# An inverse transform's first half runs ahead of the fourth block of the next forward transform

## The chip, the cores and the metric

The kernel runs on one core of one Trainium2 chip. The metric is the device time of one execution in microseconds; of several runs the median is given. Engines are named as in the profile: PE is TensorE (PEld its weight loads), DVE is VectorE, ACT is ScalarE, POOL is GpSimd, and SP is SyncE, which here only issues DMAs. TensorE's granted clock is full throughout the stretches that matter here.

## The reference, cut to what matters

There are 8 sequences of 3072 positions with 256 channels. Each goes through a circular convolution by way of the frequency domain, and the result, taken as 24,576 tokens, goes through a top-1 mixture of 8 experts, each with a capacity of 768 tokens; tokens beyond it give zero rows.

```
X = np.fft.rfft(x, axis=1);  Y = X * (filt_r + 1j * filt_i)
y = np.fft.irfft(Y, n=3072, axis=1)
tok = y.reshape(24576, 256);  logits = tok @ w_gate;  e = argmax(logits)
# the first 768 tokens of each expert are kept, in order of position
h = maximum(kept[e] @ w1[e], 0);  out[token] = softmax(logits)[e] * (h @ w2[e])
```

All data is float32.

## The kernel before, in words

**Stages.** The tokens that fill all experts come from the first three batches, so the kernel convolves three batches and then runs the experts, with a branch behind it for data where that doesn't do. The convolution of a batch has four parts. The *forward transform* (`a_rows` for the second and third batch) multiplies the input by a constant matrix A; the *middle* (`Conv.middle`) forms products with a second constant matrix out of Q (`bm`), multiplies them by the filter on VectorE and GpSimd (`b`), turns them back and adds the gate's columns on TensorE (`g`), and applies a third matrix (`bi`) into the tile V; VectorE then transposes V in four quarters (`ti`); and the *inverse* (`ai`) multiplies V by AI, evicts each result on ScalarE into a tile rt, copies the 8 gate columns into L on GpSimd, and stores the tile to ybuf in HBM by SyncE.

**The hand-over** between two batches, which happens twice, is the stretch that the change touches. In it the program issues, in this order on each engine: the forward transform of the next batch for the group of 64 frequencies (`rows_in(0)`, four blocks, called R64 in the diff), the inverse's first half (`halves[0]`, nine steps of up to three tiles of 136 columns), the forward transform for the 32 other frequencies (`rows_in(1)`, two blocks), and the inverse's second half (`halves[1]`, six steps S[0] to S[5]). Each block of `a_rows` is 64 matmul records, evicted by ScalarE in two parts into four columns of Q, from where DMAs store it to `zturn` in HBM: two of 256 KB per block by GpSimd for the 64, four of 128 KB per block by SyncE for the 32. The four blocks use columns 8 to 23 of Q, the two blocks columns 16 to 23 again. `load_Q` then brings zturn back into Q in another layout, four columns a load, six loads by SyncE; the loads 0 to 3 need all stores of the 64, the loads 4 and 5 those of the 32.

**The routing** of a batch (`route`) needs L complete: `counts` (f0 to f5, VectorE), `sums` (f6, a few small matmuls on TensorE), `slots` (f6b to f12, VectorE), then three masks (`onehot`, VectorE) and three tables (`table`, TensorE, each needs its mask and adds into one bank). It is woven by hand between the inverse's second half and the next batch's middle. The lists `fill` and `ahead` are what the next `middle` runs between its own steps: `ahead` gives one item after each `b` but the first, `fill` one list at a time.

**What sets the order.** The schedule is manual: each engine and each DMA queue does its work in the order of the program, and waits only on data and buffers. The tile rt has seven buffers, the PSUM banks for results are seven in rotation, and the masks have two buffers. A write into columns of Q waits until DMAs that read them have landed. In the second hand-over, the weights of the first expert begin to load as well (`load_a`, behind S[3] in SyncE's queue), through the tile raw and ScalarE.

Of the kernel before, what the change touches and what calls it, by code (L numbers as in the profile page):

```python
# [9 lines left out]
F32 = mybir.dt.float32  # L10
# [21 lines left out]
def dft_constants():  # L32
# [18 lines left out]
    th = tp * ((n2[:, None] * k2[None, :]) % 32) / 32  # L51
    C, S = np.cos(th), np.sin(th)
    std = np.zeros((2, 32, 2, 32))
    std[0, :, 0], std[1, :, 0], std[0, :, 1], std[1, :, 1] = C, S, -S * cj, C * cj
    inv = np.zeros((2, 32, 2, 32))
    inv[0, :, 0], inv[1, :, 0], inv[0, :, 1], inv[1, :, 1] = C.T, (-S * cj).T, S.T, (C * cj).T
    sp, isp = np.zeros((2, 32, 2, 32)), np.zeros((2, 32, 2, 32))
# [36 lines left out]
def fftconv_moe_kernel(ctx, tc, x, x0, fr, fi, fny, wg, w1, w2, ca, cai, cb, co, out, cap):  # L94
    nc = tc.nc
# [21 lines left out]
    ybuf = dram.tile([NB0, NTS, 128, CH], F32, name="ybuf")  # L117
    yall = dram.tile([NB, NTS, 128, CH], F32, name="yall")
    zturn = dram.tile([4 * NP, N2, D], F32, name="zturn")
# [3 lines left out]
    def bank():  # L123
        return psum.tile([128, 512], F32, name="ps", tag="ps")
# [45 lines left out]
    def run(fs):  # L170
        for f in fs:
            f()

    class Conv:
# [108 lines left out]
        def a_rows(self, part, t0):  # L283

            rows, r0 = PARTS[part]
            o = (8, 16)[part] + t0
            k, z = 128 // rows, self.Q[:, o:o + 4, :]
            for h in range(2):
                ps = bank()
                for i in range(2):  # L290
                    for j in range(k):
                        c, t = divmod(j * NT1[part] + t0 + 2 * h + i, 4)
                        nc.tensor.matmul(ps[j * rows:(j + 1) * rows, i * D:(i + 1) * D], self.Ac[c][:, t * QP + r0:t * QP + r0 + rows],  # L293
                                         self.xts[c][:, t, :], start=True, stop=True)
                nc.scalar.copy(z[:, 2 * h:2 * h + 2, :].rearrange("p t d -> p (t d)"), ps)
            for j in range(k):
                n2 = j * NT1[part] + t0
                (nc.sync if part else nc.gpsimd).dma_start(out=zturn[r0:r0 + rows, n2:n2 + 4, :], in_=z[j * rows:(j + 1) * rows])

        def load_Q(self, p, n):  # L300

# [124 lines left out]
        v = V[q // parts][:, q % parts * n:(q % parts + 1) * n].rearrange("p a t e -> p a e t")  # L426
        nc.vector.transpose(v, v)

    def ai(V, dst, h, L=None, parts=(1, 0)):

        c0, w = HS[h]
        k = 512 // w

        def step(part, j0, n):
            rows, r0 = PARTS[part]
            ps = bank()
            for i in range(n):
                for s in range(128 // rows):
                    o = s * NT1[part] + j0 + i
                    nc.tensor.matmul(ps[s * rows:(s + 1) * rows, i * w:(i + 1) * w], AI[:, o, r0:r0 + rows], V[h][:, :w // 2, o, :],  # L440
                                     start=True, stop=True)
            rt = p1b.tile([128, 512], F32, name="rt", tag="rt", bufs=7)
            nc.scalar.copy(rt[:, :n * w], ps[:, :n * w])  # L443
            rv = rt[:, :n * w].rearrange("p (t c) -> p t c", c=w)
            if h == 0:
                t0 = part * NT1[0] + j0
                nc.gpsimd.tensor_copy(L[:, t0:t0 + n, :], rv[:, :, 128:136])
            nc.sync.dma_start(out=dst[part * NT1[0] + j0:part * NT1[0] + j0 + n, :, c0:c0 + w].rearrange("t p c -> p t c"), in_=rv)

        return [lambda part=part, j0=j0: step(part, j0, min(k, NT1[part] - j0)) for part in parts for j0 in range(0, NT1[part], k)]  # L450
# [8 lines left out]
    def new_V(pool):  # L459
        return [pool.tile([128, n // 2, N2, 2], F32, name=f"V{c}") for c, n in VS]  # L460
# [385 lines left out]
    p1b = base_ctx.enter_context(tc.tile_pool(name="p1b", bufs=1))  # L846
# [5 lines left out]
    cv = Conv(p1b, top, side, True)  # L852
    route_tiles(p1b)

    with tc.manual_schedule():

        V = new_V(vp)
# [36 lines left out]
        fill, ahead = [[cv.finish_low]], [lambda: (cv.t(3), cv.t(4)), lambda: None, lambda: cv.t(5)]  # L894
        nz = -(-len(zfill) // (NB0 - 1))

        def with_zeros(fill, at):
            fill = [list(f) for f in fill] + [[] for _ in range(10 - len(fill))]
            for i in range(len(at)):
                fill[at[i]].append(lambda: zero_out(1))  # L900
            return fill

        def rows_in(part):
            return [lambda t0=t0: cv.a_rows(part, t0) for t0 in range(0, NT1[part], 4)]

        loads = []
        for b in range(NB0 - 1):
            fill = with_zeros(fill, (5, 6, 8) if b == 0 else (7,))
            order = [[6, 7], [], [0, 4], [1, 5], [2, 3]] if b == 0 else [[], [6, 7], [0, 4], [1, 5], [2, 3]]
            for i, cs in enumerate(order):  # L910
                fill[i] += loads[:1] + [lambda b=b, c=c: cv.load_x(b + 1, c) for c in cs]
                loads = loads[1:]
            cv.middle(V, fill, ahead)
            L = new_L()
            halves = [ai(V, ybuf[b], h, L) for h in range(2)]
            counts, sums, slots, masks, table = route(L, False, (ohp, ohp))
            Q = [lambda p=p: cv.load_Q(p, 4) for p in range(0, NP, 4)]
            for q in range(4):
                ti(V, q)
            run(rows_in(0))  # L920
            S = halves[0]
            run(S[:5] + [Q[0]] + S[5:8] + [Q[1]] + S[8:])
            interleave(rows_in(1), counts)
            S = halves[1]
            S[0]()
            sums()
            if b + 2 == NB0:
                side_ctx.close()
                w0 = run_ctx.enter_context(tc.tile_pool(name="w0", bufs=1, side="right"))
                raw0 = run_ctx.enter_context(tc.tile_pool(name="raw0", bufs=1, side="right"))  # L930
                ep = run_ctx.enter_context(tc.tile_pool(name="ep", bufs=1, side="right"))
                (load_a, cut_a), (load_b, cut_b) = (load_part(0, part, raw0, w0, 4) for part in "ab")
            run(slots)
            run([Q[2], masks[0], S[1], S[2], masks[1], Q[3], S[3], table[0]])
            if b + 2 == NB0:
                load_a()
            ahead = S[4:]
            fill = [[table[1]], [masks[2]], table[2:]]
            loads = Q[4:]


        b = NB0 - 1
# [21 lines left out]
        fill = [f + g for f, g in zip(fill + [[]] * (len(more) - len(fill)), more)]  # L964
# [11 lines left out]
        L = new_L(True)  # L976
        counts, sums, slots, masks, table = route(L, True, (ohp, ohp))
# [85 lines left out]
        with tc.If(least < cap):  # L1063
            with ExitStack() as gp:
                sm["group"] = "again"
                p1b = gp.enter_context(tc.tile_pool(name="gbase", bufs=1))
# [6 lines left out]
                V = new_V(p1b)  # L1073
# [7 lines left out]
                with tc.For_i(0, NB, 1) as b:  # L1081
# [10 lines left out]
                    L = new_L()  # L1092
                    dst = yall[bass.ds(b, 1)].rearrange("o t p c -> (o t) p c")
                    for h in range(2):
                        run(ai(V, dst, h, L))
                    counts, sums, slots, masks, table = route(L, False, (gside, gside))
# [68 lines left out]
```

## Time and profile before

| what | value |
|---|---|
| median of 3 runs | 483.5 us (481.23 to 485.53) |
| the profiled execution's own time | 478.28 us |
| its span, first to last instruction | 476.4 us |
| PE busy | 455.8 us (96%) |
| DVE, ACT, POOL busy | 242.5, 251.5, 206.8 us |
| mean granted clock of TensorE | 0.996 |
| DMA, whole span | 108.30 MB, 227 GB/s |

The busy share says how long an engine had an instruction in flight; where it stood idle, the trace names what it waited for, in brackets behind the instruction that came next. Times in the trace are from the span's start. A DMA's line shows when it was issued; its landing is listed by itself.

### The profile page before, as it was taken

The numbers are of one execution on the slowest core, as the hardware profiler recorded it, in microseconds if no ns is written. First come the engines' busy times: TensorE is split into PE (matmuls) and PEld (weight loads), VectorE is DVE, ScalarE is ACT, GpSimd is POOL, SyncE is SP. The second block draws the span as 40 slices with busy tenths as digits, with TensorE's granted clock in tenths as the row PEclk, the third lists the DMA queues.
The fourth block names the chain that finished last, engine by engine and source line by source line (L and its number), as shares of the span: only waits on it lengthen the run. The fifth ranks groups of instructions, "written<-read, shape, count | busy, mean of one in ns | idle before, by whom it ended". The sixth has DMA issues, their size and how long they took to land.

```text
span 476.4 us, 10559 instructions
## 1 busy us (share of the span) xinstructions
PE 455.8 (96%) x4125; PEld 437.9 (92%) x4125; DVE 242.5 (51%) x562; ACT 251.5 (53%) x586; POOL 206.8 (43%) x259
## 2 busy tenths in 40 slices
PE   8999997899968999998999999999999999999994
PEld 8999876899758899998999999999999999999994
DVE  4587758777578788875432432422422422423500
ACT  3555754357542887654365582582572662773411
POOL 3074240642405675247423743552561561662022
PEclk9999999999999999999999999999999999999998
DMA  8999788994899975838465989989989989993001
GB/s 316 355 296 349 283 251 270 301 250 178 239 272 300 239 164 107 227 90 167 157 156 166 200 227 274 378 190 274 373 200 276 379 201 283 364 168 97 1 25 49
DMA packets 69260, 108.30 MB, mean 227 GB/s; under 512 B 4848, under 2 KB 44496, under 8 KB 69072
## 3 DMA queue, kind: packets, MB, share of 16 engines
q1 hardware_dynamic: 51536, 72.71, 47.4%
q0 software_dynamic: 16352, 32.71, 30.8%
q10 hardware_dynamic: 1312, 2.10, 1.4%
q8 instruction: 35, 0.57, 0.5%
q14 instruction: 25, 0.20, 0.1%
HBM read 61.11 MB, written 46.40 MB: 226 GB/s over the span
## 4 chain that ended last, share of the span: by engine, by line
PE 71%; issue 9%; DMA 7%; DVE 4%; ACT 3%; POOL 3%; SPq 1%; POOLq 0%; ACTq 0%
PE ps L636 23%; PE ps L687 23%; PE ps L368 5%; PE ps L335 5%; PE ps L382 4%; PE ps L293 3%; DMA raw<-w 3%; PE ps L277 3%; PE ps L440 3%; DMA ybuf<-rt 3%; POOL y L693 2%; PE ps L610 1%; DMA V<-x 1%; DMA rows<-ybuf,idxg 1%; PE ps L322 1%
## 5 line engine op out<-in xcount | busy, mean ns | idle before, releaser
L687 PE MATMUL ps<-wbh,h 128*128 128x256 f32 x768 | 139.4, 282 | 0.0
L619 DVE SCALAR_TENSOR_TENSOR h<-ps,h 128x384 fp32r<-128x384 f32 x128 | 66.8, 552 | 106.3 <-ACT h L617 106.1
L687 PEld LDWEIGHTS ps<-wbh,h 128*128 128x128 f32 x768 | 119.1, 189 | 0.8 <-issue 0.4
L687 PE MATMUL ps<-wbl,h 128*128 128x256 f32 x384 | 107.7, 280 | 0.0
L693 POOL DMA_INDIRECT y<-ob,idxs x48 | 48.1, 1002 | 117.9 <-ACT ob L690 99.4
L636 PE MATMUL ps<-xl,wah 128*128 128x384 f32 x256 | 86.2, 337 | 0.3 <-DVE xl L621 0.2
L636 PE MATMUL ps<-xh,wah 128*128 128x384 f32 x256 | 86.3, 337 | 0.0
L636 PE MATMUL ps<-xh,wal 128*128 128x384 f32 x256 | 86.0, 336 | 0.0
L617 ACT ACTIVATE h<-ps 128x384 fp32r<-128x384 f32 x128 | 58.7, 498 | 32.9 <-PE ps L636 32.3
L687 PEld LDWEIGHTS ps<-wbl,h 128*128 128x128 f32 x384 | 72.7, 189 | 0.0
L690 ACT ACTIVATE ob<-ps,gt 128x256 f32<-128x256 f32 x48 | 22.7, 475 | 86.9 <-PE ps L687 47.3
L355 POOL TENSOR_TENSOR t<-t,t 128x256 f32<-128x256 f32 x33 | 25.2, 763 | 56.3 <-DVE t L351 44.9
L636 PEld LDWEIGHTS ps<-xl,wah 128*128 128x128 f32 x256 | 48.1, 188 | 0.9 <-DVE xl L621 0.9
L636 PEld LDWEIGHTS ps<-xh,wah 128*128 128x128 f32 x256 | 48.1, 188 | 0.2
L636 PEld LDWEIGHTS ps<-xh,wal 128*128 128x128 f32 x256 | 48.1, 188 | 0.0
L596 POOL DMA_INDIRECT rows<-ybuf,idxg x42 | 42.4, 1009 | 12.8 <-issue 11.6
L368 PE MATMUL ps<-IG,t 128*128 128x136 f32 x288 | 39.0, 282 | 1.6 <-POOL t L356 0.7
L621 DVE TENSOR_TENSOR xl<-ps,xh 128x384 fp32r<-128x384 f32 x32 | 16.2, 547 | 43.8 <-ACT xh L617 43.8
L371 ACT CAST yh<-ps 128x408 fp32r<-128x408 f32 x48 | 23.8, 504 | 27.4 <-PE ps L368 24.0
L368 PEld LDWEIGHTS ps<-IG,t 128*128 128x128 f32 x288 | 35.5, 190 | 2.9 <-POOL t L356 1.6
L335 PE MATMUL ps<-Bc,Q 128*128 128x128 f32 x288 | 36.5, 278 | 0.0
L443 ACT COPY rt<-ps 128x408 f32<-128x408 f32 (+3 forms) x40 | 20.3, 514 | 27.1 <-PE ps L440 19.7
(141 smaller groups left out, 739.7 us busy)
## 6 DMA issues: line engine op xcount, KB each, us to landing
y<-zt SPq DMA_DIRECT2D x12, 2048.0 KB, 21.7
raw<-w SPq DMA_DIRECT2D x13, 1024.0 KB, 9.7
wbl<-w POOLq DMA_DIRECT2D x16, 512.0 KB, 10.3
wal<-w POOLq DMA_DIRECT2D x14, 512.0 KB, 5.7
Q<-zturn SPq DMA_DIRECT2D x12, 512.0 KB, 6.0
ZA<-x SPq DMA_DIRECT2D x12, 384.0 KB, 12.4
zturn<-Q POOLq DMA_DIRECT2D x16, 256.0 KB, 4.5
ybuf<-rt SPq DMA_DIRECT2D x16, 256.0 KB, 5.4
```

The source lines that it names most:

```text
L335: nc.tensor.matmul(ps[:, i * 128:(i + 1) * 128], self.Q[:, p, h * 128:(h + 1) * 128], self.Bc[:, 1 if p == NP - 1 else 0, :], start=True, ...
L355: eng.tensor_tensor(out=t1[:, :, 0, :], in0=t1[:, :, 0, :], in1=t2[:, :, 1, :], op=ALU.subtract)
L368: nc.tensor.matmul(ps[:, i * 136:(i + 1) * 136], self.ysb[(p // 4, h)][:, (p % 4) * 128:(p % 4 + 1) * 128], self.IG[:, h, :], start=True, ...
L371: nc.scalar.copy(fh[:, o], ps[:, :408])
L443: nc.scalar.copy(rt[:, :n * w], ps[:, :n * w])
L596: nc.gpsimd.indirect_dma_start(out=rows[:, t, :], out_offset=None, in_=yrows[:lim, :], in_offset=bass.IndirectOffsetOnAxis(ap=idx[:, j + t ...
L617: nc.scalar.activation(out=hi, in_=ps, func=AF.Relu if relu else AF.Copy)
L619: nc.vector.scalar_tensor_tensor(out=lo, in0=ps, scalar=0.0, in1=hi.bitcast(F32), op0=ALU.max, op1=ALU.subtract)
L636: nc.tensor.matmul(ps[:, :n * 128], w[:, kk, m * 128:(m + 1) * 128], y[:, kk, o], start=k == 0, stop=k == 5)
L687: nc.tensor.matmul(ps[:, :D], y[:, m, o], w[:, m, :], start=m == 0 and j == 0, stop=m == NF - 1 and j == 2)
L690: nc.scalar.activation(out=ob, in_=ps[:, :D], func=AF.Copy, scale=gt[:, i:i + 1])
L693: ins = nc.gpsimd.indirect_dma_start(out=out, out_offset=bass.IndirectOffsetOnAxis(ap=(idxs if ix is None else ix)[:, j:j + 1], axis=0), i ...
```

## The change

The first half of the inverse is issued after three of the four blocks of 64 instead of after all four. Its first two tiles are evicted into columns 4 to 7 of Q, which the second load of Q fills later, instead of into rt. The stores of the blocks of 32 are issued by GpSimd as well. The first two loads of Q are issued behind the forward transform. The sums come ahead of S[0], S[4] moves ahead of the next middle, and the third mask moves to the place behind the first table.

```
-                (nc.sync if part else nc.gpsimd).dma_start(out=zturn[r0:r0 + rows, n2:n2 + 4, :], in_=z[j * rows:(j + 1) * rows])
+                nc.gpsimd.dma_start(out=zturn[r0:r0 + rows, n2:n2 + 4, :], in_=z[j * rows:(j + 1) * rows])
...
-    def ai(V, dst, h, L=None, parts=(1, 0)):
+    def ai(V, dst, h, L=None, parts=(1, 0), stage=()):
...
+        stage = list(stage)
...
-            rt = p1b.tile([128, 512], F32, name="rt", tag="rt", bufs=7)
+            rt = stage.pop(0) if stage else p1b.tile([128, 512], F32, name="rt", tag="rt", bufs=7)
...
-            halves = [ai(V, ybuf[b], h, L) for h in range(2)]
+            stage = [cv.Q[:, k:k + 2, :].rearrange("p k d -> p (k d)") for k in (4, 6)]
+            halves = [ai(V, ybuf[b], h, L, stage=() if h else stage) for h in range(2)]
...
-            run(rows_in(0))
-            S = halves[0]
-            run(S[:5] + [Q[0]] + S[5:8] + [Q[1]] + S[8:])
+            R64 = rows_in(0)
+            run(R64[:3] + halves[0] + R64[3:])
             interleave(rows_in(1), counts)
             S = halves[1]
-            S[0]()
-            sums()
+            run([Q[0], sums, S[0], Q[1]])
...
             run(slots)
-            run([Q[2], masks[0], S[1], S[2], masks[1], Q[3], S[3], table[0]])
+            run([S[1], masks[0], Q[2], S[2], masks[1], S[3], Q[3], table[0], masks[2], S[4]])
             if b + 2 == NB0:
                 load_a()
-            ahead = S[4:]
-            fill = [[table[1]], [masks[2]], table[2:]]
+            ahead = S[5:]
+            fill = [[table[1]], [], table[2:]]
             loads = Q[4:]
```

## Rows read from the trace of the kernel before

**Rows 1.** Windows: stretch, length, busy us (records) of PE, PEld, DVE, ACT, POOL; clock.
```profile
56.20:92.10 35.90, 31.52 (x477) 25.79 (x476) 26.21 (x50) 15.95 (x33) 12.72 (x27) 1.00 0.86 247
116.10:153.00 36.90, 31.57 (x477) 25.82 (x476) 26.33 (x50) 15.86 (x33) 12.59 (x27) 1.00 0.83 245
...
220.00:424.00 204.00, 204.00 (x1541) 202.68 (x1540) 72.06 (x191) 112.20 (x211) 97.64 (x95) 1.00 0.90 250
```

**Rows 2.** TensorE's waits, whole span: us in total, times, longest.
```profile
PE pr L576 <- DVE ohh L568: 6.7, 4, 1.7
PE pr L515 <- DVE ends L508: 3.0, 2, 2.0
...
PE ps L368 <- DVE yl L372: 0.6, 1, 0.6
```

**Rows 3.** Timeline of TensorE, first hand-over: start, us, what, [idle before, releaser].
```profile
56.29 3.88 PE L293 MATMUL ps<-ZA,A 96*64 96x256 f32 x33
...
63.35 5.97 PE L440 MATMUL ps<-V,AI 128*32 128x136 f32 x128
...
72.72 1.06 PE L440 MATMUL ps<-V,AI 128*32 128x128 f32 x32
74.83 0.17 PE L515 MATMUL pr<-ends,tri 128*128 128x8 f16 x1 [1.04 <-DVE ends L508]
...
75.05 3.00 PE L440 MATMUL ps<-V,AI 128*32 128x128 f32 x64
79.67 0.52 PE L576 MATMUL pr<-ohh,ol 128*128 128x96 f16 x8 [1.62 <-DVE ohh L568]
80.03 2.01 PE L335 MATMUL ps<-Bc,Q 128*128 128x128 f32 x16
...
90.62 0.51 PE L576 MATMUL pr<-ohh,ol 128*128 128x96 f16 x8 [1.72 <-DVE ohh L568]
90.97 1.12 PE L335 MATMUL ps<-Bc,Q 128*128 128x128 f32 x8
```

**Rows 4.** Timeline of VectorE, first hand-over.
```profile
59.08 2.50 DVE L427 STREAM_TRANSPOSE V<-V 128x2176 f32<-128x2176 f32 x1
...
72.06 0.35 DVE L483 TENSOR_REDUCE mx<-L 128x24 f32<-128x192 f32 x1 [6.08 <-POOL L L447]
...
75.16 0.17 DVE L523 COPY bs<-pr 128x16 f32<-128x16 f32 x1 [0.31 <-PE pr L518]
...
78.39 0.36 DVE L566 TENSOR_TENSOR ohh<-ioh,hif 128x384 f16<-128x384 f16 x1
```

**Rows 5.** Timeline of ScalarE, the eighth tile of the half.
```profile
70.74 0.50 ACT L443 COPY rt<-ps 128x408 f32<-128x408 f32 x1 [1.81 <-DMA ybuf<-rt]
```

**Rows 6.** Timeline of GpSimd, first hand-over.
```profile
64.36 1.03 POOL L298 DMA_DIRECT2D zturn<-Q x2 [0.71 <-ACT Q L295]
...
71.84 0.19 POOL L447 COPY L<-rt 128x8 f32<-128x8 f32 x1 [0.34 <-ACT rt L443]
82.65 0.72 POOL L355 TENSOR_TENSOR t<-t,t 128x256 f32<-128x256 f32 x1 [10.62 <-DVE t L351]
```

**Rows 7.** Timeline of SyncE's queue: the first load of Q.
```profile
70.35 1.16 SPq L303 DMA_DIRECT2D Q<-zturn  x1
```

**Rows 8.** Line L298, first hand-over: landing of GpSimd's eight stores of 256 KB.
```profile
DMA to landing us min/median/max: 3.9/4.6/5.0
```

**Rows 9.** Line L303, whole span: landing of the twelve loads of Q, 512 KB.
```profile
DMA to landing us min/median/max: 4.5/6.0/9.3
```

**Rows 10.** DMA issues, second hand-over, 124.7 to 124.9: count, KB, landing.
```profile
zturn<-Q POOLq DMA_DIRECT2D x2, 256.0 KB, 6.0
```

**Rows 11.** Timeline of TensorE, second hand-over.
```profile
135.67 0.17 PE L515 MATMUL pr<-ends,tri 128*128 128x8 f16 x1 [1.97 <-DVE ends L508]
```

**Rows 12.** Timeline of ScalarE, behind the second hand-over.
```profile
154.59 0.62 ACT L756 CAST wah<-raw 128x512 fp32r<-128x512 f32 x1 [5.20 <-DMA raw<-w]
```

**Rows 13.** Line L764, whole span: accumulating DMAs issued by GpSimd, ns min/median/max.
```profile
L764 POOL DMA_DIRECT2D wbl<-w x16: 1273/1299/1975, 171.2 to 423.4; - x16
```

## The prediction

> **What bounds the kernel now.** I read the windows first, then the waits of TensorE, then one hand-over between batches engine by engine. The windows [rows 1] show a kernel in which TensorE does not stop: from 220 to 424 us it is busy 204.00 of 204.00 us, so whatever is won earlier arrives at the end undiminished, and only TensorE's idle time can be won. The two hand-overs are where it idles: 4.4 us in the first stretch and 5.3 us in the second. The waits [rows 2] say for whom: 6.7 us in four waits of the slot table for a mask, and 3.0 us in two waits of the sums for the counts, all on VectorE. That is 9.7 us, 2.0% of the span, and is the ceiling of what this change can give. VectorE is not overloaded there: it stands idle for 6.08 us and starts the counts late, at 72.06, because the last gate column is copied at 71.84 [rows 4, 6]. That copy is late because ScalarE waited 1.81 us at its eighth tile for a store to release a buffer [rows 5].
>
> **The change, part by part, in the first hand-over.**
>
> *The inverse's first half before the fourth block.* TensorE runs the four blocks from 56.29 to 63.35, 1.76 us each [rows 3]. After three it is at 61.6; the half needs the second transpose, which starts at 59.08 and takes 2.50 [rows 4], so it starts at about 61.7. This edit costs 0.1. The half takes 5.9 (5.97 with its last matmul's tail [rows 3]) and ends at 67.6; the fourth block fills 67.6 to 69.4, and the two blocks of 32 frequencies end at 72.8 where they ended at 72.72. No matmul is added.
>
> *The two tiles in the operand.* Nine tiles against seven buffers became a wait; nine against nine leave none. No instruction is added. The last tile leaves ScalarE at about 68.3 and its gate column is copied by 68.6, against 72.03. The counts take 72.06 to 74.83, 2.8 us [rows 3, 4], so they end at 71.4, ahead of TensorE. The sums run at 72.8 without a wait: 1.04 us gone.
>
> *Sums before the half's first step.* The sums take 0.2, the next four steps of the second half 1.06 plus 3.0 (75.05 to 79.67 less the wait of 1.62) [rows 3]. TensorE is through at 77.1. VectorE begins the slots 0.33 after the sums (74.83 to 75.16) and the table follows 4.5 later (75.16 to 79.67) [rows 3, 4]: 77.7. So 0.6 of the 1.62 us remains. What is late next is again the mask.
>
> *The fifth step and the third mask.* The fifth step moves ahead of the next batch's first products; it costs its own 1.05 there and gives it back behind them. The third mask (1.2 us, 78.39 to 79.67 for such a one with its table's start [rows 3, 4]) moves into a stretch where VectorE has no product to form yet, since the first of them come at T, below. The wait of 1.72 before 90.62 [rows 3] goes. TensorE is then ready for the first products at 77.7 + 0.36 + 1.05 = 79.1, with that step done.
>
> *What becomes late: the first load of Q.* It needs the fourth block's stores. GpSimd issued them 2.75 us after the block's start (61.6 to 64.36 [rows 3, 6]); now that is 70.35, the second of the two 0.52 later, at 70.9. Landing took 3.9 to 5.0 in the first hand-over [rows 8] and 6.0 for the last two in the second [rows 10]. I take 4.3, below the median of 4.6, because the half's nine stores were issued from 63 on and are nearly through. SyncE issues the load at about 75.2 where it issued it at 70.35 [rows 7]. Loads of Q land after 4.5 to 9.3, median 6.0 [rows 9]; I take 4.8, nearest the shortest, which also was a first load. So the products start at **T = 80.1** and TensorE idles 1.0 us: the wait taken away comes back here in part.
>
> *The same landing holds ScalarE.* The last block of 32 writes the columns of Q that the fourth block's stores are reading, so its two evictions wait from about 72 to 75.2, with five evictions of the inverse behind them on ScalarE at 0.5 to 0.6 each. TensorE has seven banks and needs the first of the blocked ones only at T, so it doesn't feel this. SyncE does: the store of the first step, in front of the second load, goes out at about 77, the load at 77.5. Landing after 6.0 is 83.5; TensorE wants it at T + 2.0 + 1.05 = 83.1. I charge 0.4.
>
> *All stores by GpSimd.* Eight stores of 128 KB leave SyncE's queue and cost GpSimd 8 x 0.52 = 4.2 us [rows 6]. GpSimd was idle 10.62 us there, until 82.65 [rows 6]. The second four wait for ScalarE, go out from 76.6 to 78.7, and end before its next product at about 82.6. Nothing for that, as long as an issue stays near 0.52. The nearest dear row is an issue with accumulation, up to 1.98 [rows 13]; that is a rival below.
>
> **The sum.** The second table's last product ended at 90.97 + 1.12 = 92.1 [rows 3]. From the first product, at 80.03, that is 12.1 us, less the wait of 1.72 and the step's 1.05: 9.3. Now it ends at T + 9.3 + 0.4 = 89.8: **2.3 us gained**. The second hand-over is the same but waited 1.97 for the sums where the first waited 1.04 [rows 3, 11]: **3.2 us**. There the weights of the first expert are loaded too; ScalarE waited 5.20 us for them [rows 12] and passed 0.6 us on to TensorE [rows 2]. SyncE issues that load earlier when eight stores are gone; I take 0.5 of the 0.6. Total 6.0 of the execution's own 478.28 us (span 476.4 and 1.9 around it), 1.25%. The median of the runs, 483.5, stands 1.1% above that execution; the same share makes **477.4**.
>
> By the Trainium skill ("DMA: Bandwidth & Descriptors", Anatomy of one DMA) a transfer takes some 2 us plus its bytes at 436 GB/s; with that, an estimate, the stores would land at 74.1 and the load at 77.4, before TensorE is ready, and the sum would be that of the case "all in time" below. The landings of 3.9 and more for 256 KB [rows 8] speak against it in this stretch.
>
> **The rivals.**
>
> *All in time (0.13).* Both landings at their shortest: 70.9 + 3.9 + 4.5 = 79.3, next to TensorE's 79.1. The gains are 3.5 and 4.4, with the weights 0.6: 8.5 us, 474.9. For it: the queue is emptier than when those rows were taken. Against: the fourth block's stores share the engines with the tail of the half's.
>
> *The waits only change places (0.22).* The landings of the second hand-over: 70.9 + 6.0 + 6.0 = 82.9 for T. The first hand-over then ends at 92.2 and gains nothing, the second gains 0.8: about 482.7 us. For it: 6.0 is the median of such loads and was seen for those very stores. Against: both are rows of a queue with other stores in front.
>
> *GpSimd's issues drag (0.05).* At 1.98 [rows 13] the eight stores hold GpSimd from 72 to 88, while the next products need four subtractions and additions of 0.72 [rows 6] on it before TensorE's group at T + 5.4 = 85.5. That group then starts at about 90.8, 5.3 late; 2.6 us lost in the first and 1.7 in the second, 487.8. Against: beside the transposes such issues took 0.52 [rows 4, 6]. The Trainium skill has this as a rule ("SBUF — State Buffer", SBUF: two separate sides): while VectorE runs an operation in a two-port mode, GpSimd can't write the descriptors of its DMAs. No row here shows a stretched issue of this kind of store, so its chance is small.
>
> *The load is the bound (0.08), slower.* One mechanism: the first load, queued so late, meets the first step's store, the 32s' stores and the next loads, and lands after the longest 9.3 [rows 9] behind stores at 6.0: T = 86.2. The first hand-over ends at 95.5, 3.4 later, the second 2.5 later: 5.9 us, 489.5. It loses from T = 83.3 on, and by over 1% from 85.7. Against: the loads that took that long were issued together behind other traffic.
>
> That the edit has no effect isn't open: the buffer count decides the wait [rows 5], and the order of issue is the program's.
>
> **The numbers.** The forecast has 0.52. This kernel's measurement tells about 1% (4.8 us) from no change; the forecast's own range, T from 79.4 to 81.2, is 7.4 to 3.8 us of gain, and I count 0.05 of its chance as under 1%. Faster: 0.52 + 0.13 - 0.05 = 0.60; within 1%: 0.05 + 0.22 + 0.05 = 0.32; slower: 0.08. The range goes from all in time, with 1.5 us for the spread of the runs (481.23 to 485.53), to the case of changed places: 473.2 to 483.5.
>
> **What would show it.** In the changed trace the sums should have no wait, ScalarE none for the inverse's buffers, and the table one wait of about 0.6 us and none at the third mask. A new wait of about 1 us should stand before the first products, ended by the load of Q, and one of about 3 us on ScalarE before the last block of 32, ended by a store. The counts should start at 68.6, the first load at about 75.2. If the load is issued after 77 or takes over 6, the gain is gone; if GpSimd's issues of stores exceed 1 us, the third rival holds.

## The result, and the profile after

The changed kernel takes 484.89 us in the median of 20 runs, the kernel before 482.33 in 20 runs on the same chip. The ratio is **1.0051, with a 95% interval of 1.0031 to 1.0071**: half a per cent slower where 1.25% of gain was forecast, and above the range. (Disturbed executions are left out of every ratio here; in e12 that leaves four runs.) The profiled execution took 486.63 us with a span of 484.8, but it can't be set against that of before as a whole: its first hand-over begins at 59.38 where the other's began at 56.29 [rows 3], 3.09 us lost in the start-up, which the change does not touch. So I compare by stage, from the first matmul of a hand-over to the end of the last table's product (the third table, which the prediction's sum calls the second).

The windows of the changed kernel (stretch, length, busy us and records of PE, PEld, DVE, ACT, POOL; clock, DMA share, GB/s) are the first hand-over, a stretch inside it, and the second one:

```profile
59.30:95.80 36.50, 32.70 (x476) 26.56 (x475) 25.47 (x48) 15.75 (x33) 16.53 (x34) 0.95 0.85 235
84.70:89.90 5.20, 4.47 (x32) 3.88 (x33) 2.58 (x4) 0.59 (x1) 2.53 (x4) 0.67 0.99 296
120.00:158.60 38.60, 33.01 (x475) 27.32 (x475) 25.34 (x48) 15.76 (x33) 16.27 (x34) 0.96 0.85 237
```

Against [rows 1] one thing is new: TensorE's granted clock, 1.00 in both hand-overs before, is 0.95 and 0.96, and in the stretch behind the first products 0.67, a mixture of the two levels (from 87.20 to 89.30 it is 0.50 throughout, 1.2 of 2.4 GHz). The DMA engines, which were near full before (0.86, 0.83), are as full now. The rows also say where the time went: in the two hand-overs together TensorE stands idle for 9.4 us (length less busy time) where it stood for 9.7, but it is busy for 65.7 us where it was for 63.1, with the same matmuls.

TensorE's waits, whole span (us in total, times, longest), against [rows 2]:

```profile
PE ps L335 <- DMA Q<-zturn: 6.0, 3, 3.2
...
PE pr L577 <- DVE ohh L569: 1.5, 2, 0.7
PE ps L368 <- DVE yl L372: 1.3, 1, 1.3
PE ps L441 <- issue: 1.1, 1, 1.1
...
PE ps L335 <- ACT rt L444: 0.7, 1, 0.7
```

The 6.7 us of waits for masks have become 1.5, and the 3.0 us for the counts are gone, as forecast. In their place stand 6.0 us for loads of Q, 0.7 for an eviction at the second load, and 1.1 inside the inverse's half of the second hand-over ("issue": the trace shows nothing that TensorE waited for there). So 8.2 us of one kind are taken away and 7.8 of other kinds stand in their place, with a lower clock behind them.

TensorE's timeline in the first hand-over, to be read beside [rows 3]:

```profile
64.83 5.96 PE L441 MATMUL ps<-V,AI 128*32 128x136 f32 x128
...
76.04 0.18 PE L516 MATMUL pr<-ends,tri 128*128 128x8 f16 x1
...
80.89 0.52 PE L577 MATMUL pr<-ohh,ol 128*128 128x96 f16 x8 [0.74 <-DVE ohh L569]
...
84.72 2.57 PE L335 MATMUL ps<-Bc,Q 128*128 128x128 f32 x16 [2.28 <-DMA Q<-zturn]
87.21 1.98 PE L441 MATMUL ps<-V,AI 128*64 128x128 f32 x16
89.91 1.13 PE L335 MATMUL ps<-Bc,Q 128*128 128x128 f32 x8 [0.72 <-ACT rt L444]
...
94.47 0.51 PE L577 MATMUL pr<-ohh,ol 128*128 128x96 f16 x8
94.82 1.12 PE L335 MATMUL ps<-Bc,Q 128*128 128x128 f32 x8
```

The half starts 5.45 us after the hand-over's first matmul, the sums and the last table have no wait, and the first table waits 0.74. Then TensorE stands for 2.28 us, and its next two groups take 2.57 and 1.98 us where the same work took 2.01 and 1.10 before, at the lower clock of the window above.

The other engines at the same place, answering to [rows 4 to 7]: VectorE's counts, ScalarE's last block of 32, GpSimd's stores, SyncE's first two loads.

```profile
71.57 0.35 DVE L484 TENSOR_REDUCE mx<-L 128x24 f32<-128x192 f32 x1 [2.49 <-POOL L L448]
...
79.33 1.07 ACT L295 COPY Q<-ps 128x512 f32<-128x512 f32 x2 [4.24 <-PE ps L441]
...
73.45 1.07 POOL L298 DMA_DIRECT2D zturn<-Q  x2 [1.92 <-ACT Q L295]
...
80.70 1.93 POOL L298 DMA_DIRECT2D zturn<-Q  x4 [3.35 <-ACT Q L295]
...
79.38 0.36 SPq L303 DMA_DIRECT2D Q<-zturn  x1
...
81.38 0.48 SPq L303 DMA_DIRECT2D Q<-zturn  x1
```

The second of the fourth block's two stores goes out some 0.53 us behind the first, at 73.98, and at 79.33 and 79.38 ScalarE and SyncE, which both need it, go on together. From this I take it that it landed 5.3 us after its issue; the trace lists no landing of its own for it, and 4.0 us for the first of the two. (ScalarE's wait is put down to PE, which had long been done.) The landing of the two loads, from the DMA issues (count, KB, us to landing):

```profile
Q<-zturn SPq DMA_DIRECT2D x1, 512.0 KB, 5.2
...
Q<-zturn SPq DMA_DIRECT2D x1, 512.0 KB, 8.4
```

The second hand-over begins at 120.05. TensorE there, beside [rows 11], then the weights on SyncE and ScalarE, beside [rows 12]:

```profile
130.41 2.44 PE L441 MATMUL ps<-V,AI 128*64 128x136 f32 x37 [1.07 <-issue]
138.11 0.18 PE L516 MATMUL pr<-ends,tri 128*128 128x8 f16 x1
...
145.00 2.02 PE L335 MATMUL ps<-Bc,Q 128*128 128x128 f32 x16 [0.50 <-DMA Q<-zturn]
...
151.30 2.05 PE L335 MATMUL ps<-Bc,Q 128*128 128x128 f32 x8 [3.24 <-DMA Q<-zturn]
...
157.61 1.12 PE L335 MATMUL ps<-Bc,Q 128*128 128x128 f32 x8
...
152.76 1.19 SPq L744 DMA_DIRECT2D raw<-w  x1
...
161.09 0.62 ACT L757 CAST wah<-raw 128x512 fp32r<-128x512 f32 x1 [4.02 <-DMA raw<-w]
```

Here the inverse's half itself stands for 1.07 us, at 130.41, without a cause in the trace. The same idle time (1.0 to 1.3 us) is in the traces of e2, e3 and e9, and not in those of e4, e7 and e13, which move the same block. Then the first load is nearly in time and the second is 3.24 us late. From its start, this hand-over ends at 157.61 + 1.12 - 120.05 = 38.7 us, where before it took 36.7; the first ends at 36.6, where before it took 35.8.

### The profile page after: what moved, and what is told of

Its sections match the earlier page's. It is cut to its first block, busy times and chain, and to the rows that moved or that the text cites. A ratio compares the mean times of both kernels' runs of the same rounds, so it can differ in the third digit from the quotient of the medians.

```text
span 484.8 us, 10571 instructions
## 1 busy us (share of the span) xinstructions
PE 460.0 (95%) x4125; PEld 441.4 (91%) x4125; DVE 241.9 (50%) x562; ACT 251.0 (52%) x586; POOL 214.7 (44%) x275
## 4 chain that ended last, share of the span: by engine, by line
PE 68%; DMA 11%; issue 11%; POOL 5%; ACT 2%; DVE 1%; POOLq 1%; SPq 0%; ACTq 0%
PE ps L637 20%; PE ps L688 19%; PE ps L441 5%; PE ps L335 5%; PE ps L368 5%; PE ps L382 4%; PE ps L293 4%; DMA y<-ob,idxs 4%; PE ps L277 3%; DMA Q<-zturn 3%; POOL y L694 2%; DMA raw<-w 2%; DMA V<-x 1%; POOL rows L597 1%; PE ps L611 1%
## 5 line engine op out<-in xcount | busy, mean ns | idle before, releaser
L335 PE MATMUL ps<-Bc,Q 128*128 128x128 f32 x288 | 38.2, 285 | 6.7 <-DMA Q<-zturn 6.0
L335 PEld LDWEIGHTS ps<-Bc,Q 128*128 128x128 f32 x288 | 35.5, 199 | 7.9 <-issue 6.7
L371 ACT CAST yh<-ps 128x408 fp32r<-128x408 f32 x48 | 23.8, 506 | 32.6 <-PE ps L368 21.8
```

The source lines that it names most:

```text
L335: nc.tensor.matmul(ps[:, i * 128:(i + 1) * 128], self.Q[:, p, h * 128:(h + 1) * 128], self.Bc[:, 1 if p == NP - 1 else 0, :], start=True, ...
L371: nc.scalar.copy(fh[:, o], ps[:, :408])
```

## The experiments

All ratios are to the kernel before on the same chip in the same hour, with 95% intervals; edits are against the changed kernel unless it says "before". Hand-over lengths are quoted only where a trace supports the verdict.

**e4: the move alone.** My theory: the loss lies in the fourth block's move and the late loads behind it, not in the other edits. Against before:

```
-            run(rows_in(0))
+            R64 = rows_in(0)
-            run(S[:5] + [Q[0]] + S[5:8] + [Q[1]] + S[8:])
+            run(R64[:3] + S + R64[3:] + [Q[0], Q[1]])
```

> The kernel before with one edit: the fourth block of 64 behind the half, and the first two loads of Q behind it; nothing else. Theory 1: the first load starts 6 us later and lands at about the time of 81.5 in place of 75.4 of the first hand-over, so the first products start 1.5 us later or more, and nothing is won elsewhere, since the seven buffers still stop ScalarE: 3 to 6 us above before, ratio 1.006 to 1.012. Theory 2 (the queue of the stores matters and not the order): within 1 us of before, ratio 0.998 to 1.002.

Measured 485.16 us, **1.0053 (1.0021 to 1.0085)**: the whole loss of the change, without any of its other edits. TensorE's timeline of e4:

```profile
79.89 0.52 PE L576 MATMUL pr<-ohh,ol 128*128 128x96 f16 x8 [1.64 <-DVE ohh L568]
82.27 3.75 PE L335 MATMUL ps<-Bc,Q 128*128 128x128 f32 x16 [1.86 <-DMA Q<-zturn]
85.95 1.98 PE L440 MATMUL ps<-V,AI 128*64 128x128 f32 x16
```

The table's old wait of 1.64 us is still there and the load's 1.86 is added to it. Two idle stretches with one short group between them, and the next two groups take 3.75 and 1.98 us instead of 2.01 and 1.10. The windows of e4's two hand-overs (as above) give the same account as the changed kernel's:

```profile
57.51:96.93 39.42, 34.17 (x476) 28.00 (x476) 26.29 (x50) 15.38 (x33) 12.76 (x27) 0.91 0.81 233
121.05:158.60 37.55, 33.16 (x476) 27.15 (x476) 26.33 (x50) 15.48 (x33) 12.56 (x27) 0.95 0.81 240
```

TensorE's idle time is 9.6 us, against 9.7 before, since the waits for loads take the place of those for the counts; its busy time is 67.3 us instead of 63.1. The ratio lies just below the 1.006 to 1.012 of the theory and outside the rival's range.

**e1: everything but the move.** All four blocks run before the half again, with the first two loads inside the half, as before.

```
-            run(R64[:3] + halves[0] + R64[3:])
+            S = halves[0]
+            run(R64 + S[:5] + [Q[0]] + S[5:8] + [Q[1]] + S[8:])
-            run([Q[0], sums, S[0], Q[1]])
+            run([sums, S[0]])
```

> The changed kernel with all four blocks of 64 ahead of the half again and the first two loads of Q inside the half, as before; the two tiles in Q, the stores by GpSimd, the sums, the fifth step and the third mask stay changed. Theory 1 (the loads of Q, put off by 6 us with the fourth block's stores, ate the gain): the loads are early again, the waits for sums (1.04, 1.97 us), for the table (to about 0.6) and for the third mask (1.7 each) are won, some 3 us in each hand-over: 6 to 8 us below before, ratio 0.984 to 0.988, no wait for a load of Q on TensorE. Theory 2 (the stores of the 32 on GpSimd's queue slow the loads wherever these stand): loads of Q land after 8 us here too, TensorE waits for the second or third of them, ratio 0.995 to 1.005.

Measured 480.56 us, **0.997 (0.9941 to 0.9998)**. The sign of theory 1 was right, its size was a fifth of what I expected; the number and the late load are those of theory 2. Views of e1: TensorE, SyncE's second load, GpSimd's stores of 32, and that load's landing.

```profile
79.53 2.05 PE L335 MATMUL ps<-Bc,Q 128*128 128x128 f32 x16
...
84.97 1.66 PE L335 MATMUL ps<-Bc,Q 128*128 128x128 f32 x8 [2.35 <-DMA Q<-zturn]
...
74.88 1.19 SPq L303 DMA_DIRECT2D Q<-zturn  x1
...
72.51 3.90 POOL L298 DMA_DIRECT2D zturn<-Q  x8 [2.12 <-ACT Q L295]
...
Q<-zturn SPq DMA_DIRECT2D x1, 512.0 KB, 10.0
```

The products start on time, 22.9 us after the hand-over's first matmul. But the second load, issued among eight stores on GpSimd's queue, lands after 10.0 us, where in the trace of before the load issued there landed after 5.6, and TensorE waits 2.35.

**e2: the second load right behind the first.** Rival: the second load is late because it stands behind a store in SyncE's queue that waits for ScalarE.

```
-            run([Q[0], sums, S[0], Q[1]])
+            run([Q[0], Q[1], sums, S[0]])
```

> The changed kernel with the second load of Q issued right behind the first, no longer behind the store of the first step, which waits for ScalarE. If the place in SyncE's queue made the second load late, it is issued 1.6 us earlier, lands 1.5 us earlier, and each hand-over wins about 1.5 us: 3 us below the changed kernel, ratio to before 0.999. If the bytes in front of it decide (the stores of the 32 by GpSimd go on at the same time whatever SyncE does), it lands less than 0.5 us earlier and the ratio stays at 1.004 to 1.005.

Measured **1.0041 (1.0005 to 1.0078)**: no gain that can be told from the changed kernel's 1.0051. The place in the queue alone doesn't make the loss.

**e3: other columns for the blocks of 32.** Rival: ScalarE's wait for the late stores is what costs. The blocks of 32 write columns 8 to 15, whose stores have long landed.

```
-            o = (8, 16)[part] + t0
+            o = 8 + t0
```

> The changed kernel with the blocks of 32 evicted into columns 8 to 15 of Q instead of 16 to 23, which no unfinished store reads. ScalarE's wait of about 4 us is gone, the last four stores of the 32 go out some 3 us earlier, ahead of the first load, and the first step's store as well. If that wait made the second load late, it is issued 1.5 us earlier and each hand-over wins 1 to 2 us: ratio 0.999 to 1.001. If only the fourth block's late stores count, the first load still starts as late and the whole wins under 1 us: 1.003 to 1.005.

Measured **1.0045 (1.0015 to 1.0075)**: no gain. Views of e3 (TensorE, SyncE, GpSimd, landing of the first load):

```profile
86.39 3.75 PE L335 MATMUL ps<-Bc,Q 128*128 128x128 f32 x16 [6.48 <-DMA Q<-zturn]
...
76.89 0.36 SPq L303 DMA_DIRECT2D Q<-zturn  x1
...
72.86 3.41 POOL L298 DMA_DIRECT2D zturn<-Q  x7 [0.86 <-ACT Q L295]
...
Q<-zturn SPq DMA_DIRECT2D x1, 512.0 KB, 9.4
```

ScalarE's wait went, and with it what had held GpSimd's stores back: seven of the eight go out ahead of the first load, which then lands after 9.4 us instead of 5.2. In the changed kernel that wait of ScalarE keeps four of the eight behind the load (80.70 against 79.38).

**e6: the stores alone.** Against before, only the eight stores of 32 by GpSimd: `(nc.sync if part else nc.gpsimd)` becomes `nc.gpsimd`.

> The kernel before with one edit: the stores of the 32 by GpSimd instead of SyncE. Theory 3: they run beside the second load instead of behind it; it lands after 8 to 10 us instead of 5.6 and TensorE waits 1 to 2 us for it in each hand-over, with some work at the lower clock behind it: 2 to 5 us above before, ratio 1.004 to 1.010. Rival (the queue makes no difference, or frees SyncE): ratio 0.997 to 1.001.

Measured **0.9988 (0.9952 to 1.0024)**: nothing, either way, as the rival had it. In e6's trace the second load is issued at 73.60, just ahead of these stores, and lands after 7.1 us, at 80.7; TensorE, held until then by the waits for counts and mask, comes to it at 83.59 without a wait.

**e5: e1 with the stores of 32 back on SyncE** (the reverse edit).

> The first experiment's kernel (all four blocks first, loads of Q early) with the stores of the 32 on SyncE again, behind the first two loads. Theory 3 (two things ate the gain: the late first load, and the eight stores on the second queue, which share the DMA engines with the second load, 10.0 us to landing there): the second load lands 5.5 to 6.5 us after its issue, TensorE waits for no load, its clock stays full, and the hand-overs win 3 to 4 us each: ratio 0.984 to 0.988. Rival (the bytes are what is short, in whatever queue): some load still lands after 8 us or more and TensorE waits for it, ratio 0.994 to 1.000.

Measured **0.9958 (0.9931 to 0.9984)**: the rival's range, not theory 3's. Its second load lands like this (issued at 73.78, from the DMA issues of e5), and TensorE and ScalarE go on like this behind it and in the second hand-over:

```profile
Q<-zturn SPq DMA_DIRECT2D x1, 512.0 KB, 6.7
...
82.41 1.16 PE L335 MATMUL ps<-Bc,Q 128*128 128x128 f32 x8
...
148.67 1.80 PE L335 MATMUL ps<-Bc,Q 128*128 128x128 f32 x8 [4.44 <-DMA Q<-zturn]
...
155.40 0.62 ACT L757 CAST wah<-raw 128x512 fp32r<-128x512 f32 x1 [10.63 <-DMA raw<-w]
```

With the stores behind the loads in one queue, the second load takes 6.7 us where it took 10.0 in e1, which differs in nothing else, and is in time (no wait at 82.41). In the second hand-over the delay turns up later: a wait of 4.44 for a later load.

**e8: the routing's order alone.** Against before: the sums ahead of S[0], the fifth step and the third mask moved; no tiles in Q, no move, stores as before.

```
-            S[0]()
-            sums()
+            run([sums, S[0]])
...
-            run([Q[2], masks[0], S[1], S[2], masks[1], Q[3], S[3], table[0]])
+            run([S[1], masks[0], Q[2], S[2], masks[1], S[3], Q[3], table[0], masks[2], S[4]])
-            ahead = S[4:]
-            fill = [[table[1]], [masks[2]], table[2:]]
+            ahead = S[5:]
+            fill = [[table[1]], [], table[2:]]
```

> The kernel before with the sums ahead of the first step, the fifth step and the third mask moved as in the change, and nothing else (seven buffers for nine tiles, no tile in Q). TensorE waits for the sums 2.1 and 3.0 us, as the counts are as late as before, the table's wait falls to 0.6 and the third mask's goes: 1.7 us won in each hand-over, ratio 0.991 to 0.995. If the two tiles in Q are worth nothing, this is as fast as the kernel of the fifth experiment.

Measured 482.71 us, **0.996 (0.9928 to 0.9993)**, the same as e5, which has the two tiles in Q besides, and a little less gain than expected. ScalarE and TensorE of e8:

```profile
72.91 0.50 ACT L444 COPY rt<-ps 128x408 f32<-128x408 f32 x1 [2.74 <-DMA ybuf<-rt]
...
76.90 0.17 PE L516 MATMUL pr<-ends,tri 128*128 128x8 f16 x1 [2.76 <-DVE ends L509]
```

Without the tiles, TensorE waits 2.76 us for the sums and for no load; with them, in e5, it doesn't wait for the sums but 6.0 us, in three waits, for loads. The wait only stands in another place. And behind the 2.76 us the clock falls here too: the next 96 records, from 77.12 on, take 5.48 us, where they took 3.89 in the changed kernel (from 76.25, without a wait before them).

**e7: is it the clock?** Eight matmuls of zeros, whose results nobody uses, ahead of each of the first two groups of products, to keep TensorE busy through the waits.

```
                 if dummy and g < 2:
                     dummy(8)
```

> The changed kernel with eight matmuls of zeros, some 2 us, ahead of the first and of the second group's products in both hand-overs, results unused. If the lower clock behind the waits costs time, the waits stay under 1 us, no stretch falls below full clock, and 1 to 3 us are won against the changed kernel: ratio to before 0.999 to 1.003. If the loads alone decide, the matmuls of zeros only fill the wait, or add where it was short: 1.005 to 1.008.

Measured **1.0071 (1.0039 to 1.0103)**. TensorE's timeline of e7:

```profile
79.69 2.05 PE L880 MATMUL ps<-zt 128*128 128x128 f32 x16
81.58 1.95 PE L335 MATMUL ps<-Bc,Q 128*128 128x128 f32 x16
...
84.50 2.05 PE L880 MATMUL ps<-zt 128*128 128x128 f32 x16
87.79 1.13 PE L335 MATMUL ps<-Bc,Q 128*128 128x128 f32 x8 [1.25 <-DMA Q<-zturn]
```

The products take 1.95 again, and the mean clock of the profiled execution is 0.994 instead of 0.987. But the zeros themselves take four times 2.05 us, and the time does not fall. In the trace the two hand-overs, zeros included, take 37.1 and 36.1 us, 2.1 less in all than the changed kernel's 36.6 and 38.7. What the second wins is lost again behind it: ScalarE waits 5.70 us for the first expert's weights, TensorE 3.11 us behind that, and from the hand-over's start to the first expert it is 66.5 us against 67.4. So the time at the lower clock can be had back, but not in this way at a profit.

**e13, e14: half the bytes of each load of Q.** Rival: the hand-over is bound by bytes. `n = n // 2` in `load_Q`, so that half of Q's columns are not loaded; e13 in the changed kernel, e14 in before.

> The changed kernel with each load of Q in the hand-overs cut to two of its four columns (256 KB for 512 KB; the other columns keep old values), all else as changed. Theory 5 (the bytes on the DMA engines bound the hand-over, and the change lets the engines idle early in it): 1.5 MB fewer to move, the second load is in time, only the first is waited for by some 1 us, and the gain that was forecast appears: 5 to 8 us below before, ratio 0.983 to 0.990, and below the run with half loads of the kernel before. Theory 1 alone (the late stores and the chain behind them, whatever the bytes): the first load is still issued 6 us late, TensorE waits 1.5 to 2.5 us and its clock falls; ratio 0.996 to 1.002.

> The kernel before with the same cut of the loads. Its waits of TensorE in the hand-over are on VectorE and stay (4.4 and 5.3 us); the bytes saved only bring the first expert's weights earlier, by 2 to 4 us. Ratio 0.990 to 0.998. By theory 5 the changed kernel with half loads is 2 us or more below this one; by theory 1 alone it is above it.

Measured **1.0013 (0.9982 to 1.0043)** and **0.9994 (0.9961 to 1.0027)**. With 1.5 MB less per hand-over the loss is no longer measurable, but the gain that theory 5 expects doesn't appear; e14 shows none either, against what I expected, and the two can't be told apart. TensorE's timeline of e13 has these waits:

```profile
82.12 2.02 PE L336 MATMUL ps<-Bc,Q 128*128 128x128 f32 x16 [1.52 <-DMA Q<-zturn]
...
86.53 1.13 PE L336 MATMUL ps<-Bc,Q 128*128 128x128 f32 x8 [1.35 <-DMA Q<-zturn]
...
145.81 2.05 PE L336 MATMUL ps<-Bc,Q 128*128 128x128 f32 x8 [2.78 <-DMA Q<-zturn]
```

Loads of half the size are still late, as the chain has it (late block, its stores' landing, only then the load). That the bytes are part of it is likely, but not shown.

**e9 to e12, e15: the first expert's weights earlier.** ScalarE waited 4.02 us for them, TensorE 1.30. `load_a()` is moved ahead of the slots in four kernels: the changed one (e9), before (e10), e5 (e11), e1 (e12, and once more as e15).

> The changed kernel with the load of the first expert's weights issued before the slots in the second hand-over, ahead of the last two of the four loads of Q, not behind the fifth step's store. In every run so far TensorE reaches the first expert 26.3 to 26.7 us after ScalarE's first cut of these weights. Theory 4 (the arrival of these weights, not TensorE's waits, sets the end of the second hand-over): issued at about 143.7 in place of 152.8, they arrive 6 to 8 us earlier, the distance of 26.4 stays or grows a little as products and loads become the bound, and 3 to 7 us are won: ratio to before 0.991 to 0.999. Rival (TensorE's waits for Q set the end): the loads of Q behind the weights come 3 us later, the ratio is 1.005 to 1.011.

> The kernel before with that one edit. Theory 4: the weights are issued at about 141 in place of 146.4 and arrive 4 to 5 us earlier; 2 to 5 us won, ratio 0.990 to 0.996, although no wait of TensorE in the hand-over is touched. Rival: two loads of Q come 3 us later and nothing is won, 1.000 to 1.006.

> The fifth experiment's kernel (blocks first, early loads of Q, stores of the 32 by SyncE, the routing's order as changed) with the early weights. It won 2.2 us in the first hand-over and lost it again at the weights, which ScalarE awaited for 10.6 us. Theory 4: the weights come 5 to 6 us earlier, and 4 to 8 us below before in all: ratio 0.983 to 0.992. Rival: as the fifth experiment or slower, 0.996 to 1.002.

> The first experiment's kernel (as the last, but with the stores of the 32 by GpSimd) with the early weights. SyncE is free of eight stores, so the weights go out at about 137 in place of 147.3, and the loads of Q behind them later. Theory 4: TensorE's waits for Q grow to 3 us or more, but the weights come 8 us earlier; the end is then set by the products: 3 to 7 us below before, ratio 0.985 to 0.994. Rival: the later loads of Q cost as much as they do in the first hand-over, 0.997 to 1.003.

> The twelfth kernel again (blocks first, loads of Q inside the half, two tiles in Q, the routing's order as changed, all stores by GpSimd, the weights before the slots), for its ratio of 0.991 stood on few runs. If it was no chance: 0.988 to 0.995; if it was, 0.996 to 1.001, as its fellow with SyncE's stores.

Measured **1.0037 (1.0009 to 1.0065)**, **1.0013 (0.9984 to 1.0042)**, **1.0004 (0.998 to 1.0028)**, **0.9914 (0.9882 to 0.9946)** and **1.0003 (0.9968 to 1.0039)**. Theory 4's ranges were missed but for e12's, and e9 lies between the two. The last two are the same kernel: the gain of e12, from four runs, was not there with more, and I take e15. Elsewhere the wait moved from the weights to the loads of Q, which now stand behind 1 MB: 10.5 us in five waits in e9, 8.5 in two in e11, 3.3 in one in e10, where there had been none.

**e16: the best that these point to.** Before with e8's order, all stores by GpSimd and the weights early; no move, no tiles in Q (that is e15 without the tiles).

> The same kernel without the two tiles in Q. If the tiles' 1.8 and 2.7 us of ScalarE's wait matter, the counts are later, TensorE waits some 2 to 3 us for the sums, and it is 2 to 4 us slower than the one with them. If the DMA engines are the bound, the wait is off the path, as the eighth and fifth kernel were equal: within 1.5 us of it.

Measured 480.98 us, **0.9942 (0.9913 to 0.9971)**: faster than before, and so than the changed kernel. Against e15, taken in the same hour, it is 3.2 us faster by the medians, which neither branch of the expectation had. TensorE's waits in e16:

```profile
PE pr L516 <- DVE ends L509: 4.8, 2, 2.5
...
PE ps L335 <- DMA Q<-zturn: 1.2, 1, 1.2
```

It waits for the counts, which the change abolished, and hardly for loads. From e8 it can't be told apart.

## Why the prediction was wrong

**The edits on the engines came as forecast.** Times of the first hand-over with 3.09 taken off: the counts start at 68.5 (forecast 68.6), the table is through its wait at 77.8 (77.7), the fourth block's first store is issued at 70.36 (70.35). TensorE is ready for the products at 79.3 (79.1). The sums and ScalarE's evictions of the half have no wait for data or buffers there (in the second hand-over the half stands for the 1.07 us above). GpSimd's 32 stores take 489 to 744 ns to issue, so "GpSimd's issues drag" falls, and with it the rule of the Trainium skill ("SBUF — State Buffer", SBUF: two separate sides) as a cause here: no issue beside VectorE's work was stretched past 0.75 us. The third mask's wait is gone.

**The step that failed is "What becomes late: the first load of Q", with the 0.4 us charged for the second.** In the first hand-over:

- T was forecast at 80.1 and is 84.72 - 3.09 = 81.6: **1.5 us**. The store landed after 5.3 (I took 4.3), the load after 5.2 (4.8).
- The two groups behind the wait take 2.57 + 1.98 us, 1.5 more than the 2.01 and 1.05 of the sum. **The lower clock had no term at all**: I took the durations of an execution with the clock full throughout, and put an idle stretch in front of them.
- The second load costs 0.72 instead of 0.4: **0.3**. The profile names ScalarE's eviction, which ends at 89.87; the load landed at 89.78 (81.38 + 8.4), so that either alone would have held TensorE nearly as long.

That is 3.3 us; measured are 3.05, since the last product ends at 95.94 - 3.09 = 92.85 where 89.8 was forecast. A gain of 2.3 became a loss of 0.75.

In the second hand-over the forecast end was 36.7 - 3.2 = 33.5 us after its start, and it is 38.7: 5.1 us. T is 24.95 after the start against 23.8, **1.1**, about as much as the half's unexplained 1.07 us had put the fourth block back (the first load took only 3.7 us here, its store longer than forecast); the second load, issued at 143.1, landed after 8.0 and costs 3.24 instead of 0.4, **2.8**; the products and the table behind it, at the lower clock, take some **1.3** more (from 151.30 to the next group of another kind, at 154.98, it is 3.7 us; the same work took 2.4 before). That sums to 5.2.

The weights were credited with 0.5. They were issued 32.7 us into the hand-over instead of 30.2, since SyncE's queue waits for the late loads in front of them; ScalarE begins to cut them 0.7 us later than the hand-over's own delay explains. **The sign of that term was wrong.** And with it a premise fell, that whatever is won earlier arrives at the end undiminished: from ScalarE's first cut to the first expert it is 26.37 us in both traces (154.59 to 180.96 and 161.09 to 187.46), so what TensorE gains ahead of that counts in full only if the weights come earlier too, as e7 shows. 0.75 + 1.94 + 0.7 = 3.4 us of loss in the profiled execution, beside 2.56 in the medians; the rest of the two profiled spans' difference is the start-up's 3.09 and 1.9 us behind the first expert's start, which I can't put down to the change.

**What it rests on.** e4 shows the cause: the move and its late loads make 1.0053 by themselves. By the windows, one trace of each kernel, the loads' waits take the place of the old ones in the changed kernel and in e4, and the loss is work at the lower clock behind them. e8 shows that the gain I counted on the routing's order is real where the loads are in time, 0.4% of it. In the changed kernel it can't be had, since waits at one engine are a maximum and not a sum: TensorE, done with the routing earlier, meets a load that comes later. e1, e3 and e5 show why the price of a load was too low: 10.0 and 9.4 us for a load issued among or behind GpSimd's eight stores, 6.7 with those stores behind it in its own queue. I had taken medians of landings from a stretch with other neighbours. The Trainium skill says ("DMA: Bandwidth & Descriptors", Queues, rings and completion order) that each DMA engine serves the queues that have work in turn; these runs agree with that, without showing the turns. Its formula in Anatomy of one DMA, which is stated there for DMAs that GpSimd issues, gives, as an estimate, 2.6 us for a store of 256 KB; the fourth block's two took 4.0 and 5.3, and the measurement decides. For SyncE's loads, to which the prediction carried it over, the section has no figure; the twelve of the changed kernel took 3.7 to 9.5 us, median 8.1. I saw the DMA share of 0.86 and 0.83 in [rows 1] and did not use it: nothing in the sum priced a transfer that starts later in a stretch whose engines are nearly full. The share alone would not have given the price: it is as high in the changed kernel, where the loads' median is 8.1 us instead of 6.0.

**The rivals.** "The load is the bound" has the right sign and nearly the right place: it is the second load, not the first, that took over 8 us. It had 0.08. "The waits only change places" put T at 82.9, beyond the measured 81.6, and yet came out 2 us too fast, since it too priced neither the second load nor the clock. "All in time" falls. The measured change lies within 1%, which had 0.32 against 0.60 for faster. Two more things of the prediction don't hold. Its range doesn't follow from its own words: all in time less 1.5 us is 473.4, and the changed places are 482.7, or 484.2 with the 1.5 us; the measured time lies above either. And its sign of failure didn't come for the first load, which was issued at 76.3 and took 5.2 us, within the 77 and 6 that were named; the gain was gone all the same.

**Open.** How much of the lateness that brings the lower clock comes from bytes and how much from the chain of landings: e13 takes away, by the medians, about three quarters of the loss with half the bytes of the loads, but its interval overlaps the changed kernel's and the late loads stay. What stops TensorE for 1.07 us in the second hand-over's half is open too. With SyncE's stores the two tiles in Q make no difference that can be told (e5 against e8: 0.9958 and 0.996); with GpSimd's stores and early weights they seem to cost 0.6% (e15 against e16), with intervals that just touch.

## What to carry to other kernels

When an edit moves a producer later, write down the whole chain to the consumer (eviction, store, landing, load, landing) and price each landing by what will be in flight beside it, not by a median from another stretch. A wait taken from one engine pays only up to the next arrival, so look up how early the next operand really lands before counting the gain. And where a forecast puts an idle stretch of some microseconds in front of matmuls, give the matmuls behind it a range up to the lower clock.

## What the hardware showed that I had not expected

- After TensorE had stood for 2.28 us in the changed kernel, and for 1.64 and 1.86 us with one short group between in e4, the next groups ran at a lower granted clock: 0.67 in a window of 5.2 us, and in e4 16 records in 3.75 us instead of 2.01, near the ratio of the levels 2.4 and 1.2 GHz. So it was behind 2.76 us in e8. Behind 1.25 us (e7, 87.79), 1.29 us (e5, at 87.62: 1.13 us for 8 records) and, in the kernel before, 1.97 us [rows 11], it did not fall; the clock of that whole hand-over was 1.00 [rows 1].
- A load of 512 KB on SyncE's queue landed after 10.0 us when it was issued among eight stores of 128 KB on GpSimd's (e1), after 9.4 us behind seven of them (e3), after 7.1 us just ahead of them (e6), and after 6.7 us with the same stores behind it on its own queue (e5).
- One kernel gave 0.9914 and 1.0003 in two sets on the same chip: an interval from a few runs of one set doesn't hold all of the spread here.
